# Moving the rank product to GpSimd, and three smaller reorderings, in a top-k attention kernel with an MLP behind it

## The chip, the cores and the metric

One core of one Trainium2 chip runs the whole program in one launch. The metric is the device time of one execution in microseconds (us). Five engines work side by side, each through a queue of its own in program order: PE (TensorE: matmuls and transposes; its weight loads are shown as PEld), DVE (VectorE), ACT (ScalarE), POOL (GpSimd), and SP, which here only issues DMAs. They wait for each other by semaphores.

## The reference

Attention in which each query row keeps only its 32 largest scores, then an MLP with a PReLU:

```python
scores = (q @ k.transpose(0, 1, 3, 2)) / sqrt(64)      # q, k, v: 8 x 8 x 576 x 64, float32
kth = np.partition(scores, -32, axis=-1)[..., -32:-31] # 32nd largest of each row
scores = np.where(scores >= kth, scores, -1e9)
attn = np.exp(scores - max); attn = attn / (attn.sum() + 1e-9)
x = (attn @ v).transpose(0, 2, 1, 3).reshape(4608, 512)
h = x @ w_in                                           # 512 -> 2048
out = (np.maximum(h, 0) + alpha * np.minimum(h, 0)) @ w_out
```

## The kernel before

The 64 heads are handled as 32 pairs. A pair's score rows make 9 tiles of 128 rows by 576 columns (four per head, and a ninth that holds the last 64 rows of both heads), 288 tiles in all. The main loop has one **tick** per tile, n = 0, 1, 2 and so on, and at each tick it writes one step of every stage onto the queues, the stages being some ticks apart. Tiles 0 to 7 of a pair are taken two at a time (one **unit** of two ticks); the ninth is a unit of its own, a **single tick** (n mod 9 = 8). For the last four pairs (from tick 252 on, `N0`) the order of the tiles is another, so that the MLP of the last batch can start earlier.

What one tile goes through, with the names that the profile shows:

- PE `ps` (L331): the scores of a unit, written one unit ahead. The PSUM pool for them has room for two tiles, so the scores of a new unit wait until ACT has read the tiles before.
- ACT `b` (L340): adds an estimate of the row's threshold, `NT0`, that was worked out per pair from the second moments of k (a chain of small steps, below). ACT `h` (L346) sums the signs, which gives how many scores of a row lie above the estimate; ACT `e` (L351) is the exponential. ACT `ra` (L395) turns the counts of three tiles into the square of a rank, at every third tick.
- POOL `SG` (L356): one value per row that says on which side of the estimate the 32nd largest lies.
- DVE `y` (L362, `flip`): flips the signs of the row by `SG`, so that the wanted score is always among the largest below zero. It is the last large DVE step of a tick.
- DVE `C` (L373), `L` (L387), `C2` (L389): the 8 largest of five interleaved parts of the row, then three rounds that merge these 40 into 24 candidates in order. `L` holds those of three tiles, 72 numbers per row.
- At every third tick (n mod 3 = 2) DVE writes `EQ` (L400, `sel_eq`): a 0/1 table that has its one at the wanted rank. Then, after that tick's `y`, the **product** of `EQ` and `L` (L406, `sel_pr`), and in the next tick, behind `mk`, the **sum** over the 24 candidates into `KK` (L410, `sel_sum`). At the end of that tick (n mod 3 = 0) `KP` (L416, `limit`) turns the sum into the row limit of the three tiles, just ahead of `y`.
- Seven ticks after the scores: DVE `mk` (L436, `mask`, first in its tick) compares `b` with the limit; POOL multiplies `mk` by `e` into the weights `w` (L446); for a ninth tile there are two such products, `wm` (L446 and L452). In each tick POOL's order is `w`, then `SG` of the newest tile. `mk` and the `EQ` table have one buffer each.
- The weights are transposed by DMA (`wT`), PE multiplies them by v (`pu`, L497, in two halves per pair: `g` = 0 with four outputs of 65 columns, `g` = 1 with four and the two 64-row outputs of the ninth tile), DVE takes the reciprocal of the row sums (`rz`, L514 and, for the ninth tile, L516), and ACT scales (`xb`, `xm`, L526).

For the pair that is next to come, a chain of preparing steps is put at fixed ticks. PE transposes q (`pq`, L198) and k (`pk`, L209), each copied out of PSUM by ACT (L201, L213 `act_k`), then the last 64 rows of both (`pt`, L217 and L218, copied by L221). `pq`, `pk` and `pt` take turns in one PSUM buffer. Then come `pg` (L226), the copy `GK` (L230), `pr` (L239, in the single tick), and on DVE the small `km` (L245) and the two-part product `P` (L247, in the tick after, n mod 9 = 0), `st` on PE, and six small DVE steps (L272 to L289).

The MLP of batches that are done is cut into steps (`ph` L721, 0.9 of a tick's credit; `pz` L735 and L739, 1.5 of it) that PE takes one per tick as filling. Each has its copy on ACT (`gT` L727, `o_sb` L744), which stands at the head of the next tick's ACT work. Until tick 253 these steps have one PSUM buffer between them.

The order on PE in a tick was: scores of the next unit, where a unit begins with the next tick; one MLP step; the steps of the pair to come and `pu`.

Of the kernel before, what the change touches and what calls it, by code (L numbers as in the profile page):

```python
# [9 lines left out]
FP32 = mybir.dt.float32  # L10
BF16 = mybir.dt.bfloat16
I32 = mybir.dt.int32
AF = mybir.ActivationFunctionType
# [18 lines left out]
def kernel(  # L32
# [143 lines left out]
    def prep_plan(p):  # L176
# [117 lines left out]
        else:  # L294
            ts = [-14, -13, -12, -11, -10, -9, -7, -6, -5, -5, -4, -4, -3, -2, -8]
        dvx = "dve" if p < 2 else "dvx"
        steps = [dict(pe=[pe_q]), dict(act=[act_q], pe=[pe_k]), dict(act=[act_k], pe=[pe_t]),
                 dict(act=[act_t], pe=[pe_g]), dict(act=[act_g], pe=[pe_r]),
                 dict(dve=[dve_p]), dict(pe=[pe_s]), dict(act=[act_m]), dict(dve=[dve_2]),
                 {dvx: [dve_3]}, dict(dve=[dve_4]), {dvx: [dve_4b]}, dict(dve=[dve_5]),  # L300
# [100 lines left out]
                                iota.unsqueeze(1).to_broadcast([128, 3, KW]), ALU.is_equal)  # L401
        sel[m] = EQ

    def sel_pr(m):
        L = Ls.pop(m)
        nc.vector.tensor_tensor(L, sel[m], L, ALU.mult)  # L406
        sel[m] = L

    def sel_sum(m):
# [85 lines left out]
    def av_one(o_, d, wT, side, cs):  # L495
        for c in range(5):
            nc.tensor.matmul(o_, wT[:, 4 * side + c, cs], d["v"][:, 5 * side + c, :],  # L497
                             start=(c == 0), stop=(c == 4))

    def av(p, g):  # L500
        d = pairs[p]
        x_tiles(p // KPB)
        d["pu", g] = pu = ps_d.tile([128, 4 + 2 * g, V1], FP32, name="pu", tag="pd")
        for i in range(2):
            for side in range(2):
                av_one(pu[:, 2 * i + side, :], d, d["wT", 2 * g + i], side, slice(0, 128))
        if g == 1:
            for side in range(2):
                av_one(pu[0:64, 4 + side, :], d, d["wTm"], side, slice(64 * side, 64 * side + 64))

    def av_rz(p, g):
        d = pairs[p]
        d["rz", g] = rz = attn.tile([128, 6], FP32, name="rz", bufs=4)
        nc.vector.reciprocal(rz[:, 0:4], d["pu", g][:, 0:4, D])  # L514
        if g == 1:
            nc.vector.reciprocal(rz[0:64, 4:6], d["pu", g][0:64, 4:6, D])  # L516

    def av_out(p, g):
        d = pairs[p]
        b, kt = p // KPB, p % KPB  # L520
        pu, rz = d["pu", g], d["rz", g]
        for c in range(4 + 2 * g):
            m = 128 if c < 4 else 64
            h0 = 128 * kt + 64 * (c % 2)
            dst = xb[b][2 * g + c // 2][:, h0:h0 + 64] if c < 4 else xm[b][:, h0:h0 + 64]
            nc.scalar.activation(dst, pu[0:m, c, 0:D], AF.Copy, scale=rz[0:m, c:c + 1])  # L526

    pul = {}

# [244 lines left out]
    with tc.manual_schedule(engines={E.PE, E.Activation, E.DVE, E.Pool, E.SP}):  # L774
# [5 lines left out]
        def run(tick, eng):  # L780
            for f in cal.pop((tick, eng), ()):
                f()
# [22 lines left out]
        def tail_of(n, wn):  # L805
            wp, wj = ORDER[wn]
            b = wp // KPB
            if wp < P0:
                if wj == 3:
                    put(n + 3, "pe", lambda: av(wp, 0))  # L810
                    put(n + 4, "dve", lambda: av_rz(wp, 0))
                    put(n + 6, "act", lambda: av_out(wp, 0))
                    if wp % KPB == KPB - 1 and b >= 5:
                        put(n + 6, "end", lambda: x_turn(b, (0, 1)))
                        put(n + 8, "end", lambda: feed(b * S + 256))
                if wj == 8:
                    put(n + 4, "pe", lambda: av(wp, 1))
                    put(n + 5, "dve", lambda: av_rz(wp, 1))
                    put(n + 7, "act", lambda: av_out(wp, 1))
                    if wp % KPB == KPB - 1:  # L820
                        put(n + 7, "end", lambda: x_turn(b, range(2 if b >= 5 else 0, 5)))
                        put(n + 9, "end", lambda: feed((b + 1) * S))
            elif (wj == 8 or wj % 2) and wp % 2:
                i, g = wj // 2, (wp - P0) // 2
                dt = 2
                if i == 3 and g == 1:
                    put(n + dt, "pe", flush)
                put(n + dt, "pe", lambda: av_last(i, g))
                where = "end" if i == 3 and g == 0 else "dvx"
                put(n + dt + 1, where if where == "end" else "dve", lambda: rz_last(i, g))  # L830
                put(n + dt + 1, where, lambda: out_last(i, g))
                if i == 3:
                    if g == 1:
                        put(n + dt + 1, where, lambda: last_ph(0))
                    put(n + dt + 2 - g, where, lambda: turn_last(g))
                    if g == 1:
                        put(n + dt + 1, where, lambda: (last_ph(1), last_pz()))
                elif g == 1:
                    put(n + dt + 1, "dvx", lambda: x_turn(b, (i,)))
                    put(n + dt + 2, "end", lambda: back.extend(mlp_steps(*last.pop(i))))  # L840
# [20 lines left out]
        while n < end or back or after:  # L861
            if 8 <= n < 12:
                put(n, "end", lambda i=n - 8: load_v(1, [i]))
            for p in range(2, NPAIR):
                if n == max(0, BASE[p] - 18):
                    load(p)
                    plan(p)
                if n == max(0, BASE[p] - 13):
                    load_v(p)
            banks[0] = 2 if n >= NT else 1 if n >= N0 + 2 else 0  # L870
            if n + 1 < NT and unit_of[n + 1][2] == 0:
                scores(n + 1)
            while after:
                after.popleft()()
            if n < NT:
                n0, m, i = unit_of[n]
                if i == 0:
                    act_b(n0)
                    if m == 2:
                        run(n, "act")  # L880
                    act_s(n)
                    if m == 1:
                        run(n, "act")
                        act_e(n0)
                else:
                    act_s(n)
                    run(n, "act")
                    act_e(n0)
            run(n, "act")
            if n >= 3 and n % 3 == 0 and n - 3 < NT:  # L890
                sel_a((n - 3) // 3)
            nb = 1 if n < N0 + 2 else 2
            credit = min(credit, 0.0) + (2.4 if n >= NT else 1.9)
            first = True
            while back and credit > 0.0 and (first or nb == 2):
                pe_f, act_f, cost, takes = back[0]
                if takes and len(after) >= nb:
                    break
                back.popleft()
                pe_f()  # L900
                if act_f:
                    after.append(act_f)
                credit -= cost
                first = False
            run(n, "pe")
            if n >= NT:
                run(n, "dve")
                run(n, "dvx")
            due = wdue.get(n, ())
            for wn in due:  # L910
                if wn < NW:
                    mask(wn)
            for f in held:
                f()
            held = []
            for wn in due:
                weights(wn, wn >= NW)
                tail_of(n, wn)
            if 0 <= n - 1 < NT:
                side_of(n - 1)  # L920
            segs = seg_ops(n - LAG_S) if 0 <= n - LAG_S < NT else []
            mn = n - LAG_M
            merges = merge_ops(mn) if 0 <= mn < NT else []
            pick = bool(merges) and mn % 3 == 2
            if pick and n >= NT:
                sel_eq(mn // 3)
            lm = n - LAG_M - 3
            for i in range(max(len(segs), len(merges), 2)):
                if i < len(segs):
                    segs[i]()  # L930
                if i < len(merges):
                    merges[i]()
            run(n, "dve")
            if 0 <= lm < NT and lm % 3 == 0:
                limit(lm // 3)
            if pick and n < NT:
                sel_eq(mn // 3)
            if 0 <= n - 1 < NT:
                flip(n - 1)
            run(n, "dvx")  # L940
            if pick:
                sel_pr(mn // 3)
                held = [lambda m=mn // 3: sel_sum(m)]
                if mn % TPP == TPP - 1:
                    put(n + 2, "dve" if mn < NT - 1 else "end", lambda g=mn // TPP: check_group(g))
                    if mn == NT - 1:
                        put(n + 2, "end", checks)
                        put(n + 3, "end", final_flag)
                        put(n + 7, "end", read_flag)
            run(n, "end")  # L950
            n += 1
# [139 lines left out]
```

## Time and profile before

| what | value |
|---|---|
| median of three runs | 866.85 us (864.89 to 867.13) |
| the profiled execution | 866.57 us; its span from the first to the last instruction is 864.7 us |
| mean granted TensorE clock | 0.928 |
| DVE busy | 817.5 us, 95% of the span |
| ACT busy | 783.7 us, 91% |
| PE busy | 711.5 us, 82% |
| POOL busy | 443.6 us, 51% |

The page of a profile gives the busy time of each engine, the span in 40 slices, the chain of work that ended last, and the costliest groups of instructions. The group view has one row per line of code, engine and tile, with the number of instructions, their sum and the mean of one, and the idle time before them with what ended it. The timeline has one row per instruction: start, duration, engine, line, operation. Small DVE instructions overlap in it: the next one starts before the one ahead has ended, so what an instruction costs its engine is the distance to the next start, and not its duration. The view of waits names who waited for whom.

### The profile page before, as it was taken

The page shows a single profiled execution, that of the slowest core. Times are in us where ns is not written, and L with a number is a line of the kernel's source. Part 1 is how long each engine was busy: PE and PEld are TensorE (multiplying, and loading weights), DVE is VectorE, ACT ScalarE, POOL GpSimd, SP SyncE. Part 2 cuts the span into 40 slices and gives each one's busy share as a digit, 9 for nine tenths or more (in the row PEclk, how much of TensorE's full clock was granted, in tenths as well). Part 3 has the DMA queues.
Part 4 walks back from the last instruction along what each step waited for, and adds up shares of the span by engine and source line. Part 5 has one row for each costly group of instructions (what it writes and reads, how often), then busy time and mean ns, then how long its engine had stood idle before and what let it go on. Part 6 is the DMA issues. An engine that isn't in the chain of part 4 may idle for free. (4 is left out here: it accounts for less than half of the span.)

```text
span 864.7 us, 20335 instructions
## 1 busy us (share of the span) xinstructions
PE 711.5 (82%) x5696; PEld 424.3 (49%) x5771; DVE 817.5 (95%) x4901; ACT 783.7 (91%) x1865; POOL 443.6 (51%) x643
## 2 busy tenths in 40 slices
PE   5767688778968789877988789977897879899996
PEld 3434454434544445544454345644455455566674
DVE  5999999999999999999999999999999999998991
ACT  5989999989999999999999999999999799989861
POOL 5565555545545555554555545555555555554530
PEclk9666879889999999999997999999999899899998
DMA  7799965544775555564576456565456544435452
GB/s 144 141 162 183 168 116 102 120 97 87 137 142 119 91 116 127 108 123 90 116 162 113 96 97 130 110 126 104 100 116 126 114 100 90 94 77 96 100 91 52
DMA packets 343002, 99.06 MB, mean 115 GB/s; under 512 B 335056, under 2 KB 335328, under 8 KB 342880
## 3 DMA queue, kind: packets, MB, share of 16 engines
q1 hardware_dynamic: 338096, 94.99, 55.9%
q0 software_dynamic: 3584, 2.39, 2.2%
q8 instruction: 47, 0.77, 0.4%
q14 instruction: 75, 0.61, 0.2%
q10 hardware_dynamic: 1200, 0.30, 0.2%
HBM read 36.71 MB, written 9.44 MB: 53 GB/s over the span
## 5 line engine op out<-in xcount | busy, mean ns | idle before, releaser
L446 POOL TENSOR_TENSOR w<-mk,e 128x576 bf16<-128x576 bf16 x250 | 318.8, 1275 | 327.4 <-DVE mk L436 185.1
L373 DVE MAX8 C<-y 128x8 f32<-128x112 f32 (+1 forms) x1440 | 381.6, 265 | 0.1
L331 PE MATMUL ps<-qkT 64*128 64x288 f32 (+1 forms) x1280 | 254.1, 470 | 34.5 <-ACT b L340 33.8
L340 ACT ACTIVATE b<-ps,NT 128x576 f32<-128x576 f32 x288 | 202.1, 760 | 7.8 <-PE ps L331 7.8
L346 ACT ACTIVATE h<-b 128x576 bf16<-128x576 f32 x288 | 203.1, 705 | 1.6
L721 PE MATMUL ph<-xT,w_in_b 128*128 128x128 bf16 (+2 forms) x997 | 147.6, 289 | 41.6 <-ACT gT L727 38.4
L331 PEld LDWEIGHTS ps<-qkT 64*128 64x128 f32 (+1 forms) x1280 | 132.4, 192 | 95.4 <-ACT b L340 57.8
L351 ACT ACTIVATE e<-b 128x1152 bf16<-128x1152 f32 (+1 forms) x158 | 174.4, 1104 | 0.0
L362 DVE TENSOR_SCALAR y<-b,SG 128x576 int32<-128x576 int32 x288 | 149.4, 519 | 10.2 <-POOL SG L356 7.9
L387 DVE MAX8 L<-C 128x8 f32<-128x40 f32 x864 | 156.7, 181 | 0.1
L436 DVE TENSOR_SCALAR mk<-b,KP 128x576 bf16<-128x576 f32 x282 | 144.0, 511 | 0.0
L739 PE MATMUL pz<-w_out_b,gT 128*128 128x512 bf16 x542 | 132.6, 380 | 1.2 <-issue 0.5
L721 PEld LDWEIGHTS <-w_in_b 128*128 128x128 bf16 x1024 | 79.8, 99 | 104.2 <-issue 80.3
L727 ACT ACTIVATE gT<-ph 128x512 bf16<-128x512 f32 x140 | 85.8, 620 | 23.6 <-PE ph L721 23.4
L389 DVE MATCH_REPLACE8 C<-L,C 128x40 f32<-128x40 f32 x576 | 104.4, 181 | 0.0
L739 PEld LDWEIGHTS <-gT 128*128 128x128 bf16 x560 | 51.7, 98 | 68.9 <-issue 14.7
L497 PE MATMUL pu<-v_bf,wT 128*128 128x65 bf16 (+1 forms) x1600 | 68.8, 198 | 9.5 <-DMA wT<-w 9.1
L497 PEld LDWEIGHTS <-wT 128*128 128x128 bf16 (+1 forms) x1600 | 64.7, 103 | 18.8 <-DMA wT<-w 9.5
L356 POOL TENSOR_SCALAR SG<-S_all 128x1 int32<-128x1 f32 x288 | 64.8, 225 | 3.8 <-ACT h L346 3.5
L446 POOL TENSOR_TENSOR wm<-mk,e 128x576 bf16<-128x576 bf16 x32 | 40.8, 1276 | 46.3 <-DVE mk L436 43.7
L346 ACT ACTIVATION_READ_ACCUMULATOR h<-b 128x1 f32 x288 | 63.0, 219 | 0.0
L526 ACT ACTIVATE xb<-pu,rz 128x64 bf16<-128x64 f32 x224 | 54.4, 369 | 0.0
(116 smaller groups left out, 734.6 us busy)
## 6 DMA issues: line engine op xcount, KB each, us to landing
out_dram<-o_sb SPq DMA_DIRECT2D x34, 256.0 KB, 2.2
st_q<-in_q_dram SPq DMA_DIRECT2D x64, 128.0 KB, 2.8
kst<-in_k_dram SPq DMA_DIRECT2D x62, 128.0 KB, 2.9
st_v<-in_v_dram SPq DMA_DIRECT2D x60, 128.0 KB, 2.6
w_stage<-in_moe_w_out_dram SPq DMA_DIRECT2D x16, 256.0 KB, 3.2
w_in_b<-in_moe_w_in_dram POOLq DMA_DIRECT2D x8, 256.0 KB, 5.8
wT<-w SPq DMA_TRANSPOSE x128, 3.3
st_q<-in_q_dram SPq DMA_DIRECT2D x32, 32.0 KB, 2.6
```

The source lines that it names most:

```text
L331: nc.tensor.matmul(o_, l_, r_, start=True, stop=True)
L340: nc.scalar.activation(t["b"].rearrange("p (a c) -> p a c", a=2), t["ps"], AF.Identity, bias=NT0[:, p * TPP + j:p * TPP + j + 1], scale=ON ...
L346: nc.scalar.activation(h, tiles[n]["b"], AF.Sign, accum_out=S_all[:, n:n + 1])
L351: nc.scalar.activation(e, tiles[n0]["bu"], AF.Exp, scale=scl)
L362: nc.vector.tensor_scalar(t["y"].bitcast(I32), t["b"].bitcast(I32), FLIP, SG[:, n:n + 1], ALU.bitwise_xor, ALU.bitwise_xor)
L373: return [lambda g=g: nc.vector.max(out=C[:, n % TPP, g, :], in_=y[:, g:S // 8:NSEG, :]) for g in range(NSEG)]
L387: ops.append(lambda r=r, src=src: nc.vector.max(out=L[:, 8 * r:8 * r + 8], in_=src))
L436: nc.vector.tensor_scalar(t["mk"], t["b"], row_limit(n), None, ALU.is_ge)
L446: nc.gpsimd.tensor_tensor(dst, t["mk"], t["e"], ALU.mult)
L497: nc.tensor.matmul(o_, wT[:, 4 * side + c, cs], d["v"][:, 5 * side + c, :], start=(c == 0), stop=(c == 4))
L721: nc.tensor.matmul(hold[f][:, i, :], w_in_b[:, kk, (f + i) * 128:(f + i + 1) * 128], xT[:, kk, c0:c0 + tb], start=(kk == 0), stop=(kk == N ...
L739: nc.tensor.matmul(pz[0:m], hold["gT"][:, f, r0:r0 + m], w_out_b[:, f, :], start=False, stop=(f == NFT - 1))
```

## The change

- **Product on GpSimd, sum beside the limit.** `sel_pr` takes the engine as an argument. In ticks with n mod 3 = 0 from 6 to 288 the product is put on POOL, behind that tick's `w` (or `wm`) and ahead of its `SG`. The sum stays on DVE and moves from behind `mk` to behind the tick's last merge step, ahead of the preparing steps and of `KP`. In the last triple of tiles (n over 288) all stays on DVE.
- **One reciprocal for a second half.** The two 64-row outputs of the ninth tile share one column block of `pu`, the first in rows 0 to 63 and the second in rows 64 to 127, so that one reciprocal over five columns does for the half. ACT's two copies read those rows.
- **MLP step ahead of scores in single ticks.** In single ticks before tick 252, PE takes the MLP step first and the scores of the next unit behind it; `pr` then follows the scores.
- **k copied early.** `act_k` moves from the middle of one tick, behind the two `b`, to the very end of the tick before it, behind that tick's `e`.

```diff
-        steps = [dict(pe=[pe_q]), dict(act=[act_q], pe=[pe_k]), dict(act=[act_k], pe=[pe_t]),
+        steps = [dict(pe=[pe_q]), dict(act=[act_q], pe=[pe_k], actz=[act_k]), dict(pe=[pe_t]),
...
-    def sel_pr(m):
+    def sel_pr(m, eng):
         L = Ls.pop(m)
-        nc.vector.tensor_tensor(L, sel[m], L, ALU.mult)
+        eng.tensor_tensor(L, sel[m], L, ALU.mult)
         sel[m] = L
...
-        d["pu", g] = pu = ps_d.tile([128, 4 + 2 * g, V1], FP32, name="pu", tag="pd")
+        d["pu", g] = pu = ps_d.tile([128, 4 + g, V1], FP32, name="pu", tag="pd")
...
-                av_one(pu[0:64, 4 + side, :], d, d["wTm"], side, slice(64 * side, 64 * side + 64))
+                r = slice(64 * side, 64 * side + 64)
+                av_one(pu[r, 4, :], d, d["wTm"], side, r)
...
-        nc.vector.reciprocal(rz[:, 0:4], d["pu", g][:, 0:4, D])
-        if g == 1:
-            nc.vector.reciprocal(rz[0:64, 4:6], d["pu", g][0:64, 4:6, D])
+        nc.vector.reciprocal(rz[:, 0:4 + g], d["pu", g][:, :, D])
...
-            if n + 1 < NT and unit_of[n + 1][2] == 0:
+            nxt = n + 1 < NT and unit_of[n + 1][2] == 0
+            late = nxt and n < N0 and unit_of[n][1] == 1
+            if nxt and not late:
                 scores(n + 1)
...
+            if late:
+                scores(n + 1)
             run(n, "pe")
+            run(n, "actz")
...
+            if n >= 6 and n % 3 == 0 and n <= NT:
+                sel_pr((n - 6) // 3, nc.gpsimd)
             if 0 <= n - 1 < NT:
                 side_of(n - 1)
...
                 if i < len(merges):
                     merges[i]()
+            if n >= 6 and n % 3 == 0 and n <= NT:
+                sel_sum((n - 6) // 3)
             run(n, "dve")
...
+            if pick and n >= NT:
+                sel_pr(mn // 3, nc.vector)
+                held = [lambda m=mn // 3: sel_sum(m)]
             if pick:
-                sel_pr(mn // 3)
-                held = [lambda m=mn // 3: sel_sum(m)]
```

More of the change, by code (lines that the diff above doesn't have):

```diff
@@ L522, in av_out @@
         for c in range(4 + 2 * g):
-            m = 128 if c < 4 else 64
+            r = slice(0, 128) if c < 4 else slice(64 * (c % 2), 64 * (c % 2) + 64)
             h0 = 128 * kt + 64 * (c % 2)
             dst = xb[b][2 * g + c // 2][:, h0:h0 + 64] if c < 4 else xm[b][:, h0:h0 + 64]
-            nc.scalar.activation(dst, pu[0:m, c, 0:D], AF.Copy, scale=rz[0:m, c:c + 1])
+            c = min(c, 4)
+            nc.scalar.activation(dst, pu[r, c, 0:D], AF.Copy, scale=rz[r, c:c + 1])
     pul = {}
```

## The prediction

> **What bounds the kernel now.** I read the page first, then the busy times by stretch, then the waits, and last the timelines of DVE, POOL and PE over some ten ticks in the middle. The page gives the span and the busy times; the profiled execution took 866.57 us, 1.9 us more than its span and 0.3 us less than the median of the runs. The sum below is made against 866.57.
>
> ```profile
> span 864.7 us, 20335 instructions
> PE 711.5 (82%) x5696; PEld 424.3 (49%) x5771; DVE 817.5 (95%) x4901; ACT 783.7 (91%) x1865; POOL 443.6 (51%) x643
> ```
>
> By stretches (start and end, length, then busy us of PE, PEld, DVE, ACT, POOL, granted clock, DMA share, GB/s):
>
> ```profile
> 400.00:500.00 100.00, 83.51 (x618) 47.09 (x625) 98.20 (x596) 94.44 (x234) 51.95 (x74) 0.91 0.61 119
> 800.00:845.00 45.00, 44.73 (x490) 30.48 (x494) 44.02 (x240) 32.99 (x66) 18.10 (x26) 1.00 0.52 100
> ```
>
> In the middle DVE is busy 98.2 us of 100 and ACT 94.4; PE, at 83.5, has room. Near the end PE is full (44.7 of 45). So two stages have different bounds: up to about tick 252 the time is DVE's own list plus what DVE waits for, and in the last hundred us an edit counts only where it reaches PE. What DVE waits for, and what PE waits for, in us, times, longest:
>
> ```profile
> DVE P L247 <- PE pr L239: 10.9, 14, 1.9
> PE ps L331 <- ACT b L340: 33.8, 33, 2.8
> PE pt L217 <- ACT qkT L213: 27.1, 26, 2.4
> ```
>
> DVE's one real wait is for `pr`, 10.9 us in 14 places. The two long waits of PE are the ones that the third and the fourth edit go for; PE has room in that stage, so their price is what they take from DVE's `pr` wait, and no more.
>
> **The product.** One of the ticks that end with a limit, from the table to the next `y` (start us, duration, engine, line):
>
> ```profile
> 400.98 0.13 DVE L516 RECIPROCAL rz<-pu 64x2 f32<-64x2 f32 x1
> 401.03 0.20 DVE L400 TENSOR_TENSOR EQ<-ra,iota 128x72 f32<-128x72 f32 x1
> 401.16 0.50 DVE L362 TENSOR_SCALAR y<-b,SG 128x576 int32<-128x576 int32 x1
> 401.59 0.22 DVE L406 TENSOR_TENSOR L<-EQ,L 128x72 f32<-128x72 f32 x1
> 401.74 0.50 DVE L436 TENSOR_SCALAR mk<-b,KP 128x576 bf16<-128x576 f32 x1
> 402.17 0.21 DVE L410 TENSOR_REDUCE KK<-L 128x3 f32<-128x72 f32 x1
> 402.30 0.27 DVE L373 MAX8 C<-y 128x8 f32<-128x120 f32 x1
> ...
> 403.85 0.13 DVE L416 SCALAR_TENSOR_TENSOR KP<-KK,SG 128x3 int32<-128x3 int32 x1
> 403.91 0.50 DVE L362 TENSOR_SCALAR y<-b,SG 128x576 int32<-128x576 int32 x1
> ```
>
> The product costs DVE 0.15 us (401.59 to 401.74) and the tick, from `y` to `y`, 2.75. POOL in the same stretch, and in two later ticks with a sum:
>
> ```profile
> 402.33 1.27 POOL L446 TENSOR_TENSOR w<-mk,e 128x576 bf16<-128x576 bf16 x1 [1.29 <-DVE mk L436]
> 403.57 0.22 POOL L356 TENSOR_SCALAR SG<-S_all 128x1 int32<-128x1 f32 x1
> ...
> 410.52 1.27 POOL L446 TENSOR_TENSOR wm<-mk,e 128x576 bf16<-128x576 bf16 x1 [1.33 <-DVE mk L436]
> ...
> 412.03 0.22 POOL L356 TENSOR_SCALAR SG<-S_all 128x1 int32<-128x1 f32 x1
> ...
> 418.64 1.28 POOL L446 TENSOR_TENSOR w<-mk,e 128x576 bf16<-128x576 bf16 x1 [1.27 <-issue]
> ```
>
> POOL begins `w` 0.59 us after `mk` began (401.74 to 402.33) and gives the next instruction its turn 1.24 later. DVE, without the product and the sum in their old places, would reach the sum's new place, behind the last merge step, at about 403.57: `KP` at 403.85 less 0.15 for the product and 0.13 for the sum. The product can't start before 403.57, when `w` lets it. So DVE arrives at the sum when the product is just beginning, and waits for all of it. Behind the waiting sum are queued `KP`, the preparing steps, `y` and with it the next `mk`, for which POOL's next `w` waits; that is a loop, in which nothing else covers the wait. `SG` is also moved behind the product, and `y` needs `SG`.
>
> No row has the product on POOL. The nearest:
>
> ```profile
> L452 POOL TENSOR_TENSOR wm<-mk,e 128x64 bf16<-128x64 bf16 x32 | 9.8, 305 | 0.0
> L446 POOL TENSOR_TENSOR wm<-mk,e 128x576 bf16<-128x576 bf16 x32 | 40.8, 1276 | 46.3 <-DVE mk L436 43.7 <-DMA st_q<-in_q_dram 1.4 <-issue 1.2
> L628 POOL TENSOR_SCALAR alpha1m<-alpha_sb 128x16 f32<-128x16 f32 x1 | 0.2, 193 | 8.5 <-ACT alpha_sb L627 8.5
> L650 POOL TENSOR_SCALAR w_out_b<-w_stage,alpha1m 128x512 bf16<-128x512 f32 x5 | 8.0, 1591 | 3.1 <-DMA w_stage<-in_moe_w_out_dram 3.1
> ```
>
> The same operation takes 305 ns for 64 bfloat16 elements and 1276 for 576, so 1.90 ns for one and 184 fixed; 72 elements make 320 ns, if float32 costs the same. Lower end: the 305 of the smaller one. Upper end: the float32 rows, 193 ns for 16 elements and 1591 for 512, 2.82 ns for one: 193 + 72 x 2.82 = 396. I take 0.32, the row of the same operation and nearly the same size, and keep 0.30 and 0.40 for the range.
>
> The Trainium skill, "GPSIMD Engine Reference", section "Performance versus the Vector engine", says that a two-input elementwise operation there is held to some 2.6 cycles for one element by a single read port, twice VectorE's time, and gives 4497 ns for 2048 float32 elements. With the 184 ns above, that page would make the product about 0.34 us, an estimate, and the sum below 1.6 us longer. The same page's "When to use GPSIMD" advises against such an operation there; the traced rows agree with its slope (1.90 ns).
>
> The limit is worked out from the sum, and the two now stand next to each other. Where they did so before, at the very end:
>
> ```profile
> 840.04 0.23 DVE L410 TENSOR_REDUCE KK<-L 128x3 f32<-128x72 f32 x1
> 840.31 0.16 DVE L416 SCALAR_TENSOR_TENSOR KP<-KK,SG 128x3 int32<-128x3 int32 x1
> ```
>
> That is 0.27 us from the start of the sum to the start of `KP`. From `KP` to `y` it is 0.06 (403.85 to 403.91), and from `y` to the next large step 0.43 (401.16 to 401.59). The hand-over from POOL to DVE is 0.03, from the tick with the ninth tile, where `SG` ends at 412.03 + 0.22 and `y` starts at 412.28 (row below).
>
> First kind of tick, from `y` to `y`: 0.43 + 0.59 + 1.24 + 0.32 + 0.03 + 0.27 + 0.06 = 2.94, against 2.75: **+0.19**. By `SG` it would be 0.43 + 0.59 + 1.24 + 0.32 + 0.22 + 0.03 = 2.83, so the sum decides.
>
> Second kind, where POOL has the two products of a ninth tile:
>
> ```profile
> 409.28 0.50 DVE L362 TENSOR_SCALAR y<-b,SG 128x576 int32<-128x576 int32 x1
> 409.71 0.16 DVE L282 TENSOR_TENSOR t<-sq,t 128x9 f32<-128x9 f32 x1
> 409.79 0.21 DVE L406 TENSOR_TENSOR L<-EQ,L 128x72 f32<-128x72 f32 x1
> 409.93 0.50 DVE L436 TENSOR_SCALAR mk<-b,KP 128x576 bf16<-128x576 f32 x1
> ...
> 412.28 0.52 DVE L362 TENSOR_SCALAR y<-b,SG 128x576 int32<-128x576 int32 x1
> ```
>
> It took 3.00 us. After the change `L282` stays ahead of `mk` (0.08), and `wm` holds POOL for 1.51 (410.52 to 412.03): 0.43 + 0.08 + 0.59 + 1.51 + 0.32 + 0.03 + 0.27 + 0.06 = 3.29: **+0.29**.
>
> Third kind, the tick with `km` and `P` between the sum and the limit:
>
> ```profile
> 417.42 0.51 DVE L362 TENSOR_SCALAR y<-b,SG 128x576 int32<-128x576 int32 x1
> ...
> 417.99 0.51 DVE L436 TENSOR_SCALAR mk<-b,KP 128x576 bf16<-128x576 f32 x1
> ...
> 420.11 0.14 DVE L245 TENSOR_TENSOR km<-GK,bones 128x2 bf16<-128x2 bf16 x1
> 421.22 0.82 DVE L247 TENSOR_TENSOR P<-pr,qkT 128x512 bf16<-128x512 f32 x2 [0.97 <-PE pr L239]
> 421.96 0.15 DVE L416 SCALAR_TENSOR_TENSOR KP<-KK,SG 128x3 int32<-128x3 int32 x1
> 422.03 0.51 DVE L362 TENSOR_SCALAR y<-b,SG 128x576 int32<-128x576 int32 x1
> ```
>
> It took 4.61, of which 0.97 was the wait for `pr`: 3.64 without. After: 0.43, then 0.65 from `mk` to `w` here (417.99 to 418.64), 1.24, 0.32 and 0.03 bring the sum to 2.67; 0.13 for its turn (402.17 to 402.30); and from `km` to `y` 1.92 less 0.97. That is 3.75: **+0.11**.
>
> Together 0.59 us for a pair of heads. Product ticks before tick 252 are n = 6, 9 and so on to 249, 82 of them: 82 / 3 x 0.59 = **+16.1 us**. The price changes by 0.8 us for each hundredth of a us of the product.
>
> **One reciprocal.** L516 has its turn from 400.98 to 401.03, 0.05 us, in a tick in which nothing ahead of `y` is waiting for POOL: 28 x 0.05 = **-1.4 us**. The same matmuls and copies run on other rows; I cost that at nothing, since PE and ACT have room there. If the 64-row outputs were slower on PE, its spare 16 us in 100 would cover it.
>
> **MLP step ahead of scores, and k early.** The single tick that lies before that third tick, on PE:
>
> ```profile
> 417.98 1.24 PE L331 MATMUL ps<-qkT 64*128 64x288 f32 x6 [0.81 <-ACT b L340]
> ...
> 420.76 0.44 PE L239 MATMUL pr<-qkT,GK 64*64 64x512 bf16 x4
> ```
>
> The scores waited 0.81 us for `b`, then the step of the MLP came, then `pr`, for which DVE waited 0.97. Put into that hole the step is done when the scores can start, and `pr` follows them at least 0.81 earlier. DVE itself arrives 0.59 later with each pair. So 1.40 us are taken from waits of 0.78 on the mean (10.9 / 14) and 1.9 at the longest: I take **-10 us** of the 10.9. What could be late next is `b` of the next unit, if the step is longer than the hole; ACT has 5.6 us of 100 to give, and that is the cover. With k copied at the end of the tick before, PE no longer waits for it (27.1 us), but PE is not the bound there: nothing on its own. It could cost: ACT now stands waiting if `pk` is late, and `b`, `h` and through `SG` DVE stand behind it. `pk` follows the copy of q, and ACT has its `e` between them, so I take nothing; the bound is a few tenths a pair, inside ACT's 1.4 us of room a pair (5.6 of 100, with a pair at nine ticks of 2.75 us).
>
> **The tail.** From tick 252 on there are 12 more product ticks before tick 288, 12 x 0.19 = 2.3 us on DVE. PE is full there, so I put them at 0 and keep 2.3 for the range. A gain there I exclude: MLP work, which fills PE, is the same.
>
> **The sum.** 866.57 + 16.1 - 1.4 - 10 = 871.3 us.
>
> **Rivals.**
>
> - *The product is short (faster).* If POOL's product takes 0.225 us, no longer than 72 elements would if nearly all were fixed cost (the 193 ns row for 16 elements speaks for that, the 305 for 64 against), each of the 82 ticks gains 0.095: 871.3 - 7.8 = 863.5 us. The point from which it decides is 0.26 us: there 4.7 us are gone, and with them the loss. The same result comes if all other waits of DVE vanish along with `pr`'s. Chance 0.20.
> - *The `pr` waits stay.* If the MLP step itself waits for its PSUM buffer, and so doesn't fit the hole, PE and ACT keep the pace in the half of the pairs with a wait, and there the 0.54 is taken out of the wait; the other half pays: 866.6 + 14.7 / 2 = 873.9 us. For it speaks that the buffer is freed by ACT's `gT` in the same tick as the `b` that the scores wait for; against it that `gT` comes first. Chance 0.20.
> - *Float32 at the slow rate.* With 0.40 us for the product: 82 x 0.08 = 6.6 us more, 877.9. The L650 row speaks for it, but that operation reads a factor from a table and is another one. Chance 0.12.
> - *No effect on the pace.* ACT at 94.4 of 100 and PE in a loop with it could set the pace, with DVE's waits only a sign of it. Then both what DVE loses and what it gains is covered, and the time stays at 866.6. Against it: between `pr` waits DVE has none at all, 98.2 of 100. Chance 0.08.
>
> My forecast has 0.40. Its own range, with 0.30 to 0.34 for the product, 9 to 12 us of recovered waits and up to 2.3 in the tail, is 867.7 to 876.2. Taking the other cases in, 863 to 878. Differences under 0.3%, 2.6 us, can't be told from none here. Slower by more than that (over 869.2) are most of the forecast, the second and the third rival: 0.56. No change: the fourth rival, some of the forecast's lower end, part of the first: 0.22. Faster: the first rival and a little of what lies beside it: 0.22.
>
> **What would show it.** Right: in the ticks with a sum a wait of DVE L410 for POOL L406 of 0.2 to 0.6 us; L406 on POOL at 0.30 to 0.34 us; ticks of 2.94, 3.29 and 3.75; the `pr` wait under 3 us; PE's wait of `pt` for the copy of k gone. Wrong: a sum that doesn't wait, which would need a product that starts before `w` is done or is over in 0.1; `pr` waits still at 10 us; or new waits of ACT for `pk` or the scores that are longer than a us a pair.

## The result, and the profile after

The changed kernel takes **875.52 us** (median of four runs, 873.39 to 876.95) against 866.00 for the kernel before in the same series: ratio 1.0099, 95% interval 1.0080 to 1.0118. It is slower by one per cent. The forecast was 871.3 us, slower, with 863 to 878 as its range. The profile is of the slowest of the four runs, 876.95 us, so the spans below differ by 10.5 us where the medians differ by 9.5.

Head of the page of the changed kernel, then the groups of the moved product, of the sum and of `P` (busy us, mean ns | idle time before, and what ended it):

```profile
span 875.2 us, 20275 instructions
PE 708.5 (81%) x5696; PEld 425.2 (49%) x5771; DVE 812.8 (93%) x4778; ACT 796.2 (91%) x1865; POOL 472.3 (54%) x738
```

```profile
L406 POOL TENSOR_TENSOR L<-EQ,L 128x72 f32<-128x72 f32 x95 | 32.2, 339 | 0.0
L410 DVE TENSOR_REDUCE KK<-L 128x3 f32<-128x72 f32 x96 | 21.9, 228 | 22.5 <-POOL L L406 17.6
L247 DVE TENSOR_TENSOR P<-pr,qkT 128x512 bf16<-128x512 f32 x64 | 26.1, 448 | 1.9 <-PE pr L239 1.9
```

The row of the sum in the kernel before:

```profile
L410 DVE TENSOR_REDUCE KK<-L 128x3 f32<-128x72 f32 x96 | 20.8, 216 | 0.1
```

VectorE has become less busy, 812.8 us instead of 817.5, while the span grew by 10.5. The product costs GpSimd 339 ns. The sum has 22.5 us of idle time ahead of it, where it had 0.1, and `P` has 1.9 where it had 10.9. The mean granted TensorE clock of the profiled execution went from 0.928 to 0.910. What part of the time goes with that was not taken apart, but the longer ticks below are not made by it: from 400 to 500 us, where they stand, it is 0.93, against 0.91 before. Who waited for whom, in us, times, longest:

```profile
DVE KK L410 <- POOL L L406: 17.6, 59, 0.4
ACT qkT L213 <- PE pk L209: 13.7, 12, 7.0
PE pt L217 <- ACT qkT L213: 7.2, 10, 0.9
```

The wait for the product is new. PE's wait of `pt` for the copy of k has gone from 27.1 to 7.2 us, and a new one has come the other way round: ACT stands 13.7 us before that copy, waiting for `pk`, 7.0 of it at one place.

A tick of the first kind on DVE, from `y` to `y`, with the sum and the limit at its end, and POOL beside it (last two rows: the tick with a ninth tile):

```profile
410.10 0.51 DVE L362 TENSOR_SCALAR y<-b,SG 128x576 int32<-128x576 int32 x1
410.53 0.51 DVE L436 TENSOR_SCALAR mk<-b,KP 128x576 bf16<-128x576 f32 x1
...
412.74 0.23 DVE L410 TENSOR_REDUCE KK<-L 128x3 f32<-128x72 f32 x1
413.00 0.16 DVE L416 SCALAR_TENSOR_TENSOR KP<-KK,SG 128x3 int32<-128x3 int32 x1
413.08 0.51 DVE L362 TENSOR_SCALAR y<-b,SG 128x576 int32<-128x576 int32 x1
```

```profile
411.13 1.28 POOL L446 TENSOR_TENSOR w<-mk,e 128x576 bf16<-128x576 bf16 x1 [1.09 <-DVE mk L436]
412.36 0.34 POOL L406 TENSOR_TENSOR L<-EQ,L 128x72 f32<-128x72 f32 x1
412.66 0.23 POOL L356 TENSOR_SCALAR SG<-S_all 128x1 int32<-128x1 f32 x1
...
419.56 1.28 POOL L446 TENSOR_TENSOR wm<-mk,e 128x576 bf16<-128x576 bf16 x1 [1.29 <-DVE mk L436]
...
421.05 0.34 POOL L406 TENSOR_TENSOR L<-EQ,L 128x72 f32<-128x72 f32 x1
```

The product starts 1.23 us behind `w`, the sum 0.38 behind the product, the limit 0.26 behind the sum: 2.98 us in all, 2.75 before. The other two kinds of tick:

```profile
418.44 0.52 DVE L362 TENSOR_SCALAR y<-b,SG 128x576 int32<-128x576 int32 x1
...
421.43 0.23 DVE L410 TENSOR_REDUCE KK<-L 128x3 f32<-128x72 f32 x1 [0.41 <-POOL L L406]
421.57 0.17 DVE L285 TENSOR_REDUCE sq<-t 128x9 f32<-128x27 f32 x1
421.69 0.16 DVE L416 SCALAR_TENSOR_TENSOR KP<-KK,SG 128x3 int32<-128x3 int32 x1
421.77 0.52 DVE L362 TENSOR_SCALAR y<-b,SG 128x576 int32<-128x576 int32 x1
...
426.90 0.51 DVE L362 TENSOR_SCALAR y<-b,SG 128x576 int32<-128x576 int32 x1
...
429.59 0.23 DVE L410 TENSOR_REDUCE KK<-L 128x3 f32<-128x72 f32 x1 [0.20 <-POOL L L406]
429.73 0.15 DVE L245 TENSOR_TENSOR km<-GK,bones 128x2 bf16<-128x2 bf16 x1
429.80 0.82 DVE L247 TENSOR_TENSOR P<-pr,qkT 128x512 bf16<-128x512 f32 x2
430.53 0.15 DVE L416 SCALAR_TENSOR_TENSOR KP<-KK,SG 128x3 int32<-128x3 int32 x1
430.60 0.52 DVE L362 TENSOR_SCALAR y<-b,SG 128x576 int32<-128x576 int32 x1
```

They take 3.33 and 3.70 us (3.00, and 3.64 without its `pr` wait, before). In the latter, `P` follows `km` without a wait, where 0.97 us stood before.

Taken over pairs 1 to 27, the median ticks with a sum are 2.98, 3.32 and 3.70, against 2.75, 3.01 and 3.63 before; the tick with the reciprocal of a second half is 2.62 against 2.68, and the other five are the same to 0.01. When `y` of some tiles starts, and the span, in us:

| kernel | tile 18 | tile 251 | tile 287 | span |
|---|---|---|---|---|
| before | 67.5 | 730.1 | 833.6 | 864.7 |
| changed | 72.7 | 739.5 | 844.6 | 875.2 |
| difference | +5.2 | +9.4 | +11.0 | +10.5 |

Half of the loss is there before the twentieth tile. It comes in two places, and the first is already 1.74 us long at tile 6, when no product's wait has yet cost anything. There ACT takes the first of the early copies of k:

```profile
25.48 1.17 ACT L351 ACTIVATE e<-b 128x1152 bf16<-128x1152 f32 x1
28.26 0.59 ACT L213 COPY qkT<-pk 128x512 f32<-128x512 f32 x1 [1.62 <-PE pk L209]
```

`e` ends at 26.65, and ACT stands for 1.62 us until `pk`, which PE does behind the scores of the next unit. At the second place, on PE and then on ACT of the changed kernel:

```profile
54.35 0.73 PE L497 MATMUL pu<-v_bf,wT 128*128 128x65 bf16 x10 [6.43 <-DMA wT<-w]
55.02 2.29 PE L331 MATMUL ps<-qkT 64*128 64x288 f32 x8
57.64 0.63 PE L661 MATMUL pl<-xT,w_inT 128*128 128x512 bf16 x1 [0.33 <-issue]
58.07 1.02 PE L209 MATMUL pk<-ident_f,kst 128*128 128x128 f32 x4
```

```profile
50.89 1.21 ACT L351 ACTIVATE e<-b 128x1152 bf16<-128x1152 f32 x1
59.13 0.59 ACT L213 COPY qkT<-pk 128x512 f32<-128x512 f32 x1 [7.02 <-PE pk L209]
```

PE waits 6.43 us for the transposed weights of the first pair. The scores and a product that prepares the MLP's weights come next, and `pk` behind them. ACT has nothing queued ahead of the copy of k, so it stands from 52.1 to 59.1, with the two `b` behind it whose scores (55.02, 2.29 us long) were there nearly two us earlier. In the kernel before, the two `b` came first, and ACT waited 2.99 us for their scores:

```profile
53.95 1.37 ACT L340 ACTIVATE b<-ps,NT 128x576 f32<-128x576 f32 x2 [2.99 <-PE ps L331]
55.21 0.59 ACT L213 COPY qkT<-pk 128x512 f32<-128x512 f32 x1
```

Not all of the 7.02 us is the copy's. PE's wait for these weights was 4.79 us before, 4.8 to 5.2 in the three runs below that also copy k early from the start, and 4.5 to 6.05 in those that copy it late there; ACT's wait at this place was 5.5 to 5.8 us in those three.

### The profile page after: what moved, and what is told of

Same layout as the page of the kernel before. It is cut to its first block, busy times and chain, and to the rows that moved or that the text cites. A ratio compares the mean times of both kernels' runs of the same rounds, so it can differ in the third digit from the quotient of the medians.

```text
span 875.2 us, 20275 instructions
## 1 busy us (share of the span) xinstructions
PE 708.5 (81%) x5696; PEld 425.2 (49%) x5771; DVE 812.8 (93%) x4778; ACT 796.2 (91%) x1865; POOL 472.3 (54%) x738
## 5 line engine op out<-in xcount | busy, mean ns | idle before, releaser
L331 PE MATMUL ps<-qkT 64*128 64x288 f32 (+1 forms) x1280 | 243.1, 472 | 21.3 <-ACT b L340 20.9
L346 ACT ACTIVATE h<-b 128x576 bf16<-128x576 f32 x288 | 199.2, 692 | 2.2
L331 PEld LDWEIGHTS ps<-qkT 64*128 64x128 f32 (+1 forms) x1280 | 130.3, 194 | 80.2 <-ACT b L340 36.2
L721 PEld LDWEIGHTS <-w_in_b 128*128 128x128 bf16 x1024 | 81.8, 100 | 120.1 <-issue 94.1
L727 ACT ACTIVATE gT<-ph 128x512 bf16<-128x512 f32 x140 | 84.8, 614 | 13.1 <-PE ph L721 12.7
L739 PEld LDWEIGHTS <-gT 128*128 128x128 bf16 x560 | 51.9, 98 | 69.7 <-issue 16.1
L346 ACT ACTIVATION_READ_ACCUMULATOR h<-b 128x1 f32 x288 | 59.1, 205 | 0.0
```

The costliest lines, as they stand in the source:

```text
L331: nc.tensor.matmul(o_, l_, r_, start=True, stop=True)
L346: nc.scalar.activation(h, tiles[n]["b"], AF.Sign, accum_out=S_all[:, n:n + 1])
L721: nc.tensor.matmul(hold[f][:, i, :], w_in_b[:, kk, (f + i) * 128:(f + i + 1) * 128], xT[:, kk, c0:c0 + tb], start=(kk == 0), stop=(kk == N ...
L739: nc.tensor.matmul(pz[0:m], hold["gT"][:, f, r0:r0 + m], w_out_b[:, f, :], start=False, stop=(f == NFT - 1))
```

## The experiments

The first four undo one part of the change each, or move one. Ratios are to the kernel before in the same series, whose median was 867.15 us in the first, 866.21 in the second and 867.39 in the third.

**k late** (the changed kernel without its fourth edit)

```diff
-        steps = [dict(pe=[pe_q]), dict(act=[act_q], pe=[pe_k], actz=[act_k]), dict(pe=[pe_t]),
+        steps = [dict(pe=[pe_q]), dict(act=[act_q], pe=[pe_k]), dict(act=[act_k], pe=[pe_t]),
```

> The changed kernel with the copy of k put back to where it was before, behind the two b of the next tick. In the profile of the changed kernel the first 19 ticks lose 5.15 us against before, of which five product ticks explain about 1 us; in that stretch ACT stood 7.0 us before one copy of k, waiting for pk. Theory: the early copy costs about 4 us at the start and brings nothing later, so this kernel takes 871.5 us, and the start of tick 19's y comes back to within 1.5 us of before. Rival: the start is lost because weights come later and PE waits longer for their transposes (6.4 us in one place against 4.8); then nothing is gained, 875.5. Second rival: k copied late brings back PE's wait for it and with it waits of DVE for pr: 878 or more.

Measured: 871.02 us, 1.0049 (1.0032 to 1.0067). `y` of tile 18 starts at 67.2 us, 0.3 before its time in the kernel before, and nothing is lost later: the theory held to half a microsecond.

**Product on VectorE** (the changed kernel without its first edit)

```diff
-            if n >= 6 and n % 3 == 0 and n <= NT:
-                sel_pr((n - 6) // 3, nc.gpsimd)
...
-            if n >= 6 and n % 3 == 0 and n <= NT:
-                sel_sum((n - 6) // 3)
...
-            if pick and n >= NT:
+            if pick:
                 sel_pr(mn // 3, nc.vector)
                 held = [lambda m=mn // 3: sel_sum(m)]
```

> The changed kernel with the product back on VectorE and the sum back behind mk; the single reciprocal, the MLP order and the early copy of k stay. Theory: the product's move alone costs 0.61 us a pair (ticks of 2.98, 3.32 and 3.70 go back to 2.75, 3.01 and 3.59), 16.7 us to tick 252, and the waits for pr stay away because PE has pr ready earlier: 875.5 - 16.7 = 858.8 us, with under 3 us of waits for pr. Rival: the waits for pr went only because DVE had become slower; then they come back with 8 to 11 us, and the time is about 868.

Measured: 867.17 us, 1.0005 (0.9989 to 1.0021). The rival was right. Its waits:

```profile
ACT qkT L213 <- PE pk L209: 12.5, 11, 5.8
DVE P L247 <- PE pr L239: 10.1, 14, 2.0
```

The ticks are back at 2.75 and 3.01, and 10.1 us of waits for `pr` are back too. So in the changed kernel they were gone in part because DVE came later.

**Product ahead of `w`** (the same product on GpSimd, placed before the mask of its tick)

```diff
+            if n >= 6 and n % 3 == 0 and n <= NT:
+                sel_pr((n - 6) // 3, nc.gpsimd)
             due = wdue.get(n, ())
             for wn in due:
                 if wn < NW:
                     mask(wn)
...
-            if n >= 6 and n % 3 == 0 and n <= NT:
-                sel_pr((n - 6) // 3, nc.gpsimd)
```

> The changed kernel with the product ahead of w on GpSimd instead of behind it: it then runs in the 1.1 us in which GpSimd waits for mk. The sum stays behind the merges. Theory: the sum no longer waits and SG is no longer behind the product; ticks of about 2.74, 2.87 and 3.49 in place of 2.98, 3.32 and 3.70, so 0.9 us a pair or 24 us less to tick 252: about 851 us. Rival, from the Trainium skill, SBUF - State Buffer, section on the two separate sides: GpSimd and a VectorE instruction of a two-port kind exclude each other for their whole length, and y and mk, which run just then, may be such; then y or mk is held up by the product, 0.3 us in each of 82 ticks, and the time is about 871 to 876.

Measured: 867.60 us, 1.0007 (0.9991 to 1.0023). Neither number. The sum no longer waits; the ticks are 2.82, 3.01 and 3.70, and 12.2 us of waits for `pr` have come back, as in the run before this one. DVE and POOL around such a product:

```profile
405.10 0.20 DVE L400 TENSOR_TENSOR EQ<-ra,iota 128x72 f32<-128x72 f32 x1
405.21 0.52 DVE L362 TENSOR_SCALAR y<-b,SG 128x576 int32<-128x576 int32 x1
405.64 0.60 DVE L436 TENSOR_SCALAR mk<-b,KP 128x576 bf16<-128x576 f32 x1
```

```profile
405.45 0.48 POOL L406 TENSOR_TENSOR L<-EQ,L 128x72 f32<-128x72 f32 x1 [0.29 <-DVE EQ L400]
406.32 1.28 POOL L446 TENSOR_TENSOR w<-mk,e 128x576 bf16<-128x576 bf16 x1 [0.40 <-DVE mk L436]
```

Here the product overlaps `y` and `mk`. It takes 0.48 us instead of 0.34, `mk` 0.60 instead of 0.51, and `y` its 0.52 as ever. The Trainium skill ("SBUF — State Buffer", the section on its two separate sides) says that GpSimd and a VectorE instruction of a two-port kind exclude each other for their whole length. The rows agree in part: the product and `mk` get longer when they meet. But the two overlap by 0.29 us (405.64 to 405.93), `mk` loses 0.09 of it and the product 0.14, and `y` loses nothing; an exclusion for the whole length is not shown. Whether `y` and `mk` are of that kind no run here tells.

**MLP step behind the scores** (the changed kernel without its third edit)

```diff
-            late = nxt and n < N0 and unit_of[n][1] == 1
+            late = False
```

> The changed kernel with the scores of the next unit back ahead of the MLP step in single ticks. Theory: DVE comes 0.6 us later with each pair than before, so only part of the waits for pr returns, 2 to 5 us: 878 to 880 us. Rival: the slower DVE alone took the waits away: 875.5, no change. Other rival: the MLP order is the only cause, and all 11 us of waits come back: 885.

Measured: 889.38 us, 1.0263 (1.0235 to 1.0291), beyond all three. Its waits:

```profile
ACT gT L727 <- PE ph L721: 24.2, 24, 2.4
ACT qkT L213 <- PE pk L209: 13.1, 11, 5.5
DVE P L247 <- PE pr L239: 14.5, 14, 2.3
```

The first of these stood at 23.4 us before and at 12.7 in the changed kernel. With the early copy of k and the old MLP order both, `pr` is later than ever, although DVE comes later too.

So the four edits do not add up, and the second series took them apart.

**One reciprocal and the MLP order alone** (product on VectorE, k late: the first two diffs above together)

> The kernel before with two of the four edits alone: one reciprocal, and the MLP step ahead of the scores in single ticks. Product and sum are on VectorE in their old places, k is copied late. Against e2 only the copy of k differs. Theory after the first four runs: with the faster DVE list ACT and PE set the pace (in e2 ACT is busy 97 of 100 us and DVE waits 10 us for pr), and the early copy costs ACT 12 us of standing before the copy of k. Without it: 4.5 us less than e2, as e1 was less than the changed kernel, 862 to 863 us. Rival: the MLP order alone takes the waits for pr away, and they had come back in e2 only through the early copy; then 867 - 11 - 4 = 853 to 856. Other rival: PE's wait for the late copy (27 us in before) costs as much as ACT's wait for pk: 867.

Measured: 859.43 us, 0.9913 (0.9894 to 0.9932), between theory and rival. The wait for `pr`, and the busy times from 100 to 700 us of the kernel before and of this one (PE, PEld, DVE, ACT, POOL):

```profile
DVE P L247 <- PE pr L239: 4.0, 6, 1.8
```

```profile
100.00:700.00 600.00, 501.96 (x3884) 287.07 (x3943) 589.20 (x3564) 569.77 (x1393) 316.28 (x448) 0.95 0.58 115
```

```profile
100.00:700.00 600.00, 506.23 (x4016) 291.14 (x4017) 596.73 (x3595) 587.09 (x1412) 321.13 (x453) 0.93 0.59 117
```

The wait has gone from 10.9 to 4.0 us without the product's move and without the early copy. Against the run with the early copy it is 7.7 us faster. DVE is busy 99.5 of 100 us where it was 98.2, ACT 97.9 where it was 95.0: ACT now has 2 of 100 us to spare.

**Product ahead of `w`, k late** (the first and the third diff together)

> As e3 (product ahead of w on GpSimd, sum behind the merges), with k copied late. In e3 the ticks with a sum were 2.82, 3.01 and 3.70 in place of 2.98, 3.32 and 3.70, and 12 us of waits for pr had come back. Theory: k late gives 4.5 us again, 863. Rival: ACT's waits for pk were what brought the waits for pr back; then another 8 us go and it is 855.

Measured: 858.28 us, 0.9901 (0.9882 to 0.9920). 3.5 us of waits for `pr` are left. Its time can't be told from that of the run before it.

**Product behind `w`, k late, MLP behind the scores** (the product's move and the one reciprocal alone: the first and the fourth diff together)

> The changed kernel with k copied late and the MLP step back behind the scores: so the product's move (and the single reciprocal) alone. e4, which had the early copy too, took 889. Theory: the early copy and the old MLP order together made e4 slow, each pushing PE's queue later; without either, DVE's longer list swallows half of the waits for pr: 866.5 + 15.3 - 5 = 877. Rival: the MLP order alone is worth the 14 us between e4 and the changed kernel; then 871 + 14 = 885. Other rival: a slower DVE never waits for pr: 871, as e1.

Measured: 879.48 us, 1.0172 (1.0146 to 1.0197), near the theory. 7.2 us of waits for `pr` are left.

**Product ahead of `w`, sum behind `mk`, k late** (the run two above, with the sum moved)

```diff
             for f in held:
                 f()
             held = []
+            if n >= 6 and n % 3 == 0 and n <= NT:
+                sel_sum((n - 6) // 3)
...
-            if n >= 6 and n % 3 == 0 and n <= NT:
-                sel_sum((n - 6) // 3)
```

> As e6, with the sum back behind mk, where it stood before the change. The product is over by then (in e3 at 405.93, with mk's turn ending at 406.17), so the sum doesn't wait, and it no longer stands right ahead of the limit, which saves 0.13 us in two ticks of three. Theory: DVE's list is then the shortest of all, about 2.69, 2.96 and 3.57, but ACT and PE set the pace: within 2 us of e6. Rival: DVE's list still counts: 0.32 us a pair, 9 us under e6.

Measured: 858.81 us, 0.9908 (0.9888 to 0.9928). The first kind of tick is down to 2.69, and the time is the same within what can be told; 5.8 us of waits for `pr` stand where 3.5 stood. So DVE's list no longer sets the time by itself.

The times of the combinations side by side, with the sum where the changed kernel has it or, with the product on VectorE, where it was (one reciprocal in all but the first):

| product | copy of k | MLP step | us | ratio |
|---|---|---|---|---|
| VectorE (before) | late | behind scores | 866.0 to 867.4 | 1 |
| VectorE | late | ahead | 859.4 | 0.9913 |
| VectorE | early | ahead | 867.2 | 1.0005 |
| GpSimd, behind `w` | late | behind | 879.5 | 1.0172 |
| GpSimd, behind `w` | late | ahead | 871.0 | 1.0049 |
| GpSimd, behind `w` | early | behind | 889.4 | 1.0263 |
| GpSimd, behind `w` (changed) | early | ahead | 875.5 | 1.0099 |
| GpSimd, ahead of `w` | early | ahead | 867.6 | 1.0007 |
| GpSimd, ahead of `w` | late | ahead | 858.3 | 0.9901 |

Two last runs put the price of the product and of the early copy to the test.

**k early from the sixth pair on** (late for the first five)

```diff
-        steps = [dict(pe=[pe_q]), dict(act=[act_q], pe=[pe_k], actz=[act_k]), dict(pe=[pe_t]),
+        steps = [dict(pe=[pe_q]), dict(act=[act_q], pe=[pe_k], **({} if p < 5 else dict(actz=[act_k]))),
+                 dict(pe=[pe_t], **(dict(act=[act_k]) if p < 5 else {})),
```

> The changed kernel with k copied late for the first five pairs and early for all others. Theory: the 4.5 us between the changed kernel (875.5) and e1 (871.0) are lost in the first 19 ticks, where PE stands waiting for the first transposed weights with pk queued behind it, and ACT waits for pk; with the late copy there it is 871 us, and y of tick 19 is within 1.5 us of before's. Rival: the early copy costs a little in every pair; then most of it stays, 874.

Measured: 870.73 us, 1.0044 (1.0024 to 1.0064); `y` of tile 18 at 68.0 us. That is the time of the run with k late throughout, 871.02. In the changed kernel the whole cost of the early copy lies in the first pairs, and from there on it brings nothing either. `y` of tile 6 starts at 32.1 us here and at 33.8 in the changed kernel, so 1.7 of the 4.7 us at tile 18 come from the first early copy.

**The product twice** (k late)

```diff
+        if eng is nc.gpsimd:
+            spare = attn.tile([128, 3, KW], FP32, name="spare", bufs=1)
+            eng.tensor_tensor(spare, sel[m], L, ALU.mult)
         eng.tensor_tensor(L, sel[m], L, ALU.mult)
```

> As e1 (the changed kernel with k copied late), with the product done twice on GpSimd, the first time into a spare tile; the result is the same. Theory: the product stands in a closed loop, so each of the 82 ticks before tick 252 and the 12 after it grows by the 0.30 to 0.34 us of one more product, less what is left of waits for pr (under 1 us): 871 + 25 to 28 = 896 to 899 us. Rival: ACT's and PE's pace swallows a good part, as it swallowed 5 us of the first product (871.0 of e1 against 859.4 of e5, 11.6, where the ticks grew by 16.7); then under 888.

Measured: 903.58 us, 1.0421 (1.0390 to 1.0452): 32.6 us more than with one. The two on POOL:

```profile
414.14 0.34 POOL L408 TENSOR_TENSOR spare<-EQ,L 128x72 f32<-128x72 f32 x1
414.56 0.34 POOL L409 TENSOR_TENSOR L<-EQ,L 128x72 f32<-128x72 f32 x1
```

The second waits for the first and starts 0.42 us behind it, not 0.30 to 0.34. The three kinds of tick grow by 0.42, 0.41 and 0.36, and 82 / 3 x 1.19 = 32.5 us. All of it is paid: in this arrangement nothing covers the product, so the theory held and only its size was off.

## Why the prediction was right, and where it was not

- *DVE's list bounds the middle; the sum waits for POOL.* Right. The steps of 0.19, 0.29 and 0.11 us measured 0.23, 0.31 and 0.07. For 82 ticks that makes 16.7 us; 16.1 was forecast. The run with the product twice shows the loop itself.
- *The product takes 0.32 us, 0.30 to 0.40.* It measured 0.339. The row of the same operation in bfloat16 was a little low; the estimate from the Trainium skill's page ("GPSIMD Engine Reference", "Performance versus the Vector engine"), 0.34, was the better one. The prediction has the traced rows agree with the slope of the Trainium skill's page; its 4497 ns for 2048 elements make 2.2 ns for one, an estimate, a sixth above the rows' 1.90. The upper end was worked out wrongly: 193 ns is the whole of 16 elements, so 56 more at 2.82 make 351 for 72, and not 396. The third rival would then have stood at 873.8 us, and not at 877.9.
- *One reciprocal, -1.4 us.* 0.06 us in each such tick, 1.7 for 28.
- *The waits for `pr`, -10 us.* 10.9 went to 1.9. The reason given had two halves, an earlier `pr` and a later DVE, and both were needed: with the MLP order alone 4.0 us stay, with the product's move alone 7.2. The range for this term, 9 to 12, reached above the 10.9 that there was. What the step did not see is that the early copy brings the waits back where DVE is faster: 10.1 us with the product on VectorE, against 4.0 with the same lists and k late. By which step on PE it does so was not followed up.
- *k early costs nothing; its bound is a few tenths a pair.* **Wrong, and this is the step that failed.** I reasoned from a pair in the middle, where `pk` follows the copy of q and `e` covers it. In the first pairs nothing covers it: `pk` comes 1.62 us after `e` has ended in the first, and in the second PE's queue stands for the weights' transposes, and ACT behind it for 7.0 us. The sign that was named for this, more than a us a pair, would not have caught it: 13.7 us over the whole span are 0.4 a pair, but 8.6 of them are in two. The edit costs 4.5 us in the changed kernel, 7.7 with the product on VectorE, and 8 to 10 with the MLP step behind the scores. A queue that an instruction is moved past has to be looked at over the whole span, not in a typical stretch.
- *The tail at 0, up to 2.3.* From tile 251 to 287 1.6 us came on. Which part of it is DVE's was not taken apart.
- *Sum.* 16.7 - 1.7 - 9.0, with 4.1 at the start (5.2 less some 1.0 for the five products there) and 1.6 in the tail, is 11.7; the spans differ by 10.5. The rest was not taken apart. The forecast had 4.7, half of the 9.5 between the medians; the two terms put at nothing, the start and the tail, add 5.7. That the time still lies within the range is in part luck: its upper end was set by a slower product, fewer recovered waits and the tail, and not by the start.
- *The rivals.* A short product and a slow one are both ruled out by the 339 ns. "The `pr` waits stay" was not what happened in the changed kernel; whether its reason, an MLP step that waits for its PSUM buffer, is behind the waits of the other runs was not looked into. Part of "no effect on the pace" is real: between the runs with 871.0 and 859.4 us (both with one reciprocal, k late and the MLP step ahead) the product's move costs 11.6 us and not 16.7. From tile 18 to tile 251, with 77 of the 82 ticks, 15.7 us were due and 12.0 came; there 3.5 us of DVE's waits for `pr` and 0.7 of `y`'s for `SG` stand in the faster run, and none in the slower one. So other engines take back part of what DVE gains. That ACT, at 97.9 of 100, is the one that sets the pace then is likely, but not shown.

## What to carry to other kernels

Before moving a small operation to an engine with idle time, ask where in that engine's order it stands: behind the instruction that a tight loop passes through most of it is paid (11.6 of 16.7 us here, and all of a second product), and ahead of it, in the time in which the engine waits anyway, it cost nothing that could be told here. A copy moved earlier to release one engine makes the other stand for its input; look for the place where that input is latest, which was the start here. And undo the parts of a change one by one: two of the four edits here, the MLP order and the reciprocal, are worth 0.9% alone, and the other two ate it twice over.

## What the runs showed of the hardware that was not expected

A product of 72 float32 elements takes GpSimd 339 ns, against a turn of 0.15 us on VectorE; beside VectorE's `y` and `mk` it takes 0.48, `mk` grows from 0.51 to 0.60, and `y` does not grow. A GpSimd instruction that doesn't wait for the one ahead starts some 0.04 us before that one's end (the product behind `w`, 412.36 against 411.13 + 1.28); one that waits for it starts 0.08 after (414.56 against 414.14 + 0.34).
